# Head-wise attention backward on one core: ScalarE's order around the exponential, and the queue of the first weight loads

## The chip, the cores and the metric

One Trainium2 chip, one core of it. The metric is device microseconds of one execution, the median of several; lower is better. The kernel before took 420.46 us (three runs, 419.29 to 421.68).

## What is computed

One token passes a layer that mixes a cached attention block and a dense block with a gate, and the gradients of everything but `B_x` are returned with it. All tensors are bf16; `x` is 640 wide, there are 32 heads of 128, and each head's cache holds 4096 keys and 4096 values.

```python
def _A_ref(x, k_cache, v_cache, wq, wo):
    q = (x @ wq).reshape(B, Sq, H, Dh).transpose(0, 2, 1, 3)
    scores = einsum("bhqd,bhkd->bhqk", q, k_cache) * (Dh ** -0.5)
    p = softmax(scores)
    o = einsum("bhqk,bhkd->bhqd", p, v_cache)
    return o.transpose(0, 2, 1, 3).reshape(B, Sq, H * Dh) @ wo

g = sigmoid((x * gate_w).sum(-1))
out = g * _A_ref(...) + (1 - g) * _B_ref(...)      # _B_ref: w1, bias, Mish, w2
_out, _vjp = jax.vjp(_f, A_x, A_k_cache, A_v_cache, A_wq, A_wo, B_w1, B_b1, B_w2, gate_w)
return (_out, *_vjp(grad_out))
```

The large data are K and V in (32 MB each) and dK and dV out (32 MB each). For one head, dV is the outer product of the probabilities p with the gradient of the head's output, and dK that of ds = p * (dP - D) with the scaled query, where dP = V · dO.

## The kernel before

**Tiling.** A head's K (or V) is one SBUF tile of 128 partitions by 32 rows by 128 elements, 1 MB, loaded by one DMA on SP's queue. There are four buffers for K, three for V, and four for finished outputs `o_sb` (1 MB each). Four heads make a group; a group has a 640 KB slice of `wq` and one of `wo`.

**One head.** `tr_block` turns a quarter of K or V (8 of the 32 rows) with TensorE into one of two PSUM buffers `tr`, and ScalarE copies that to `KT` or `VT` (line 449). So V of a head is four blocks, `v_tr(h, 0)` to `v_tr(h, 3)`, and block 2 can only be transposed once block 0 is copied out. `scores` multiplies KT with the query; VectorE takes the row maximum `m` and ScalarE makes the diagonal `dgm` of it. `softmax` lets TensorE spread the maxima (`mx`, line 480), VectorE reduce them to `negM` (line 482), and ScalarE take the exponential `e_bf` (line 485), with a second short instruction that reads its row sum into `zd`. `dP` multiplies VT with dO on TensorE; VectorE's `pj` (line 492) multiplies dP with `e_bf`. `zd_mm` (line 496) sums over the partitions, `probs` (lines 500 to 506) makes p and ds, `dv_out` and `dk_out` make the outputs with two VectorE products each (line 511) and store each 1 MB with one DMA on SP's queue. `dq_o` (line 534) reads K and V once more on TensorE, and `dqo_red` (line 543) collects its result.

**The order around the change.** The order is written by hand: each engine runs its instructions in the order of the program's text. In the loop over the heads (from line 623) it is: V blocks 0 and 1, `softmax(h)` with the exponential, `dk_out(h - 1)`, for the first head of a group `g_dobc` (one TensorE product and one ScalarE copy to `do_row`), V blocks 2 and 3, `dP(h)`, K blocks 0 and 1 of the next head, `zd_mm`, `probs`, K blocks 2 and 3, `dv_out`, `scores(h + 1)`, `dq_o(h)`, then the loads of K four heads on and V three heads on, and then `dqo_red` and other work that fills in (weight gradients of the group before, the dense block). On ScalarE, the copies of V blocks 2 and 3 therefore stand behind the exponential, which waits for VectorE's `negM`. The last head stands by itself (from line 709) with the same order.

**Start.** SP issues the two halves of K of head 0 (line 130), then V of 0, K of 1, V of 1, K of 2, `wq` and `wo` of group 1, V of 2, K of 3, and the dense weights. POOL issues `wq` and `wo` of group 0 (lines 131 and 132), then a small bias load, and after these it makes the identity matrix (lines 153 and 154) and clears buffers. The first use of `wq` is `g_qcol(0)` (line 585), the query columns of group 0; nearly all that follows on TensorE and VectorE in the prologue stands behind it. The first use of `wo` is `g_do(0, hh)` (lines 614 and 615, instruction in line 219), four VectorE reductions, one per head, that give dO; the row maximum of head 0 stands behind them on VectorE.

Of the kernel before, what the change touches and what calls it, by code (L numbers as in the profile page):

```python
# [16 lines left out]
def kernel(  # L17
# [24 lines left out]
    nc = tc.nc  # L42
# [66 lines left out]
    def load_v(h):  # L109
        if h < H:  # L110
            vts[h] = kv_in.tile([P, J, Dh], BF16, name="Vn", tag="Vn", bufs=VBUFS)
            nc.sync.dma_start(vts[h][:], Vv[h])

    def load_wq(g, eng):
        wqs[g] = wts.tile([P, RC, GD], BF16, name="wq_g", tag="wq_g")
        eng.dma_start(wqs[g][:], wq_v[:, :, g * GD:(g + 1) * GD])

    def load_wo(g, eng):
        wos[g] = wts.tile([P, G, D], BF16, name="wo_g", tag="wo_g")
        eng.dma_start(wos[g][:], wo_v[:, g * G:(g + 1) * G, :])  # L120
# [7 lines left out]
    kts[0] = kv_in.tile([P, J, Dh], BF16, name="Kn", tag="Kn")  # L128
    for c in range(2):
        nc.sync.dma_start(kts[0][:, c * JH:(c + 1) * JH, :], Kv[0][:, c * JH:(c + 1) * JH, :])  # L130
    load_wq(0, nc.gpsimd)
    load_wo(0, nc.gpsimd)
    load_v(0)
    load_k(1)
    load_v(1)
# [80 lines left out]
    def g_do(g, hh):  # L216
        gp = groups[g]
        junk = small.tile([P, D], BF16, name="junk", tag="junk", bufs=2)
        nc.vector.scalar_tensor_tensor(junk[:], in0=wos[g][:, hh, :], scalar=1.0, in1=da_bc[:],  # L219
                                       op0=ALU.mult, op1=ALU.mult, accum_out=gp["do_col"][:, hh:hh + 1])  # L220
# [17 lines left out]
    def g_dobc(g):  # L238
        g_bcast(groups[g]["do_diag"], groups[g]["do_row"], 0, G)
# [11 lines left out]
    def f_bc(g, a=0, b=G):  # L251
        g_bcast(groups[g]["dq_diag"], groups[g]["dq_bc"], a, b)

    def f_aT_pe(g, a=0, b=G):
        gp = groups[g]
        gp["aT_ps"] = grp([P, RC], F32, "aT_ps")
        for c in range(RC):
            for hh in range(a, b):
                nc.tensor.matmul(gp["aT_ps"][:, c:c + 1], lhsT=wos[g][:, hh, c * P:(c + 1) * P],
                                 rhs=gp["o_bf"][:, hh:hh + 1], start=(hh == a), stop=(hh == b - 1))  # L260
# [4 lines left out]
    def f_dx(g, c, a=0, b=G, slot=None):  # L265
        gp = groups[g]
        cs = slice(a * Dh, b * Dh)
        slot = g if slot is None else slot
        junk = small.tile([P, D], BF16, name="junk", tag="junk", bufs=2)
        nc.vector.scalar_tensor_tensor(junk[:, cs], in0=wqs[g][:, c, cs], scalar=1.0, in1=gp["dq_bc"][:, cs],  # L270
                                       op0=ALU.mult, op1=ALU.mult, accum_out=dx_parts[:, c, slot:slot + 1])
# [172 lines left out]
    def tr_block(src, dst, c):  # L444
        sl = slice(c * TB, (c + 1) * TB)
        tp = tr_ps.tile([P, TB, P], BF16, name="tr", tag="tr")
        for t in range(TB):
            nc.tensor.transpose(tp[:, t, :], src[:, c * TB + t, :], ident_bf[:])  # L448
        nc.scalar.copy(dst[:, sl, :].rearrange("p a b -> p (a b)").bitcast(F32),  # L449
                       tp[:].rearrange("p a b -> p (a b)").bitcast(F32))  # L450

    def cols_mm(out, T, zrow):
        for j in range(J):
            nc.tensor.matmul(out, lhsT=T[:, j, :], rhs=zrow[:, J - 1 - j:2 * J - 1 - j],  # L454
                             start=(j == 0), stop=(j == J - 1))

    def k_tr(h, c):
        if h < H:
            if c == 0:
                KT[h] = kvT.tile([P, J, P], BF16, name="KT", tag="KT")  # L460
            tr_block(kts[h], KT[h], c)

    def v_tr(h, c):
        if c == 0:
            VT[h] = kvT.tile([P, J, P], BF16, name="VT", tag="VT")
        tr_block(vts[h], VT[h], c)
# [11 lines left out]
    def softmax(h):  # L478
        mx = s_ps.tile([P, P + 2], F32, name="mx", tag="mx")
        nc.tensor.matmul(mx[:, 0:P], lhsT=scale_f[:], rhs=dgms.pop(h)[:], start=True, stop=True)  # L480
        negM = small.tile([P, 1], F32, name="negM", tag="negM")
        nc.vector.tensor_reduce(negM[:], mx[:, 0:P], axis=AX.X, op=ALU.max, negate=True)  # L482
        es[h] = small.tile([P, J], BF16, name="e_bf", tag="e_bf")
        zds[h] = small.tile([P, 2], F32, name="zd", tag="zd")
        nc.scalar.activation(es[h][:], S_ps.pop(h)[:], ACT.Exp, bias=negM[:], scale=scale, accum_out=zds[h][:, 0:1])  # L485
        return mx

    def dP(h):
        DP_ps[h] = s_ps.tile([P, J], F32, name="DP", tag="DP")
        cols_mm(DP_ps[h][:], VT.pop(h), doz[h // G % 2][:, h % G, :])  # L490
        pj = small.tile([P, J], F32, name="pj", tag="pj")
        nc.vector.scalar_tensor_tensor(pj[:], in0=DP_ps[h][:], scalar=1.0, in1=es[h][:],
                                       op0=ALU.mult, op1=ALU.mult, accum_out=zds[h][:, 1:2])

    def zd_mm(h, mx):
        nc.tensor.matmul(mx[:, P:P + 2], lhsT=ones_f[:], rhs=zds[h][:], start=True, stop=True)
# [19 lines left out]
    def out_pair(h, dst, col4, row):  # L516
        hh = h % G
        t = outs.tile([P, J, Dh], BF16, name="o_sb", tag="o_sb")
        for a in (0, JH):
            outer(t, col4, row[:, hh * Dh:(hh + 1) * Dh], a, a + JH)  # L520
            if h == H - 1:
                nc.sync.dma_start(dst[h][:, a:a + JH, :], t[:, a:a + JH, :])
        if h < H - 1:
            nc.sync.dma_start(dst[h], t[:])
# [4 lines left out]
    def dk_out(h):  # L529
        out_pair(h, dKv, ds4s[h], groups[h // G]["qs_row"])  # L530
# [92 lines left out]
    for h in range(H - 1):  # L623
        g, hh = h // G, h % G
        nx, pv = g + 1 < NG, g > 0
        v_tr(h, 0)
        v_tr(h, 1)
        mx = softmax(h)
        if h > 0:
            dk_out(h - 1)  # L630
        if hh == 0 and pv:
            g_dobc(g)
        v_tr(h, 2)
        v_tr(h, 3)
        dP(h)
        if hh == 0 and pv:
            f_bc(g - 1)
            f_aT_pe(g - 1)
        k_tr(h + 1, 0)
        k_tr(h + 1, 1)  # L640
        zd_mm(h, mx)
        if hh == 0 and pv:
            f_dx(g - 1, 0)
        if hh == 1 and pv:
            f_dx(g - 1, 3)
        if hh == 2 and nx:
            g_do(g + 1, 0)
        if hh == 3 and nx:
            g_do(g + 1, 3)
        probs(h, mx)  # L650
        k_tr(h + 1, 2)
        k_tr(h + 1, 3)
        dv_out(h)
        scores(h + 1)
        od = dq_o(h)
        load_k(h + KBUFS)
        load_v(h + VBUFS)
        dqo_red(h, od)
        budget = 0.0
        if hh == 0:  # L660
            if nx:
                g_new(g + 1)
            if pv:
                f_aT_add(g - 1)
                f_dx(g - 1, 1)
                f_dx(g - 1, 2)
                f_dwo(g - 1, 0)
                f_dwo(g - 1, 1)
            budget = 2.7
        if hh == 1:  # L670
            if pv:
                f_dx(g - 1, 4)
                for c in range(RC):
                    f_dwq(g - 1, c)
                f_dwq_st(g - 1)
                f_dwo(g - 1, 2)
                f_dwo(g - 1, 3)
                f_dwo_st(g - 1)
            if g + 2 < NG:
                load_wq(g + 2, nc.gpsimd if pv else nc.sync)  # L680
                load_wo(g + 2, nc.gpsimd if pv else nc.sync)
            budget = 1.8
        if hh == 2:
            if nx:
                g_do(g + 1, 1)
                g_do(g + 1, 2)
                g_qcol(g + 1)
            budget = 2.7
        if hh == 3:
            if nx:  # L690
                g_docol(g + 1)
                g_dodiag(g + 1)
                g_q(g + 1)
                g_qs(g + 1)
                f_new(g)
                f_diag(g)
            budget = 1.8
        if h >= 2:
            mlp_some(budget)
            dw2_some(2)  # L700
        if h == H - 4:
            assert not mq and dw2_next[0] == FCN
            nc.gpsimd.dma_start(dw1_v, w1_sb[:])
            for a, b in W2P:
                nc.gpsimd.dma_start(dw2_v[:, a:b, :], w2_sb[:, a:b, :])
            nc.gpsimd.dma_start(out_8[FM:F, :], w2_sb[0:FT, FR, :])
            nc.sync.dma_start(db1_row, dh_bc[0:1, :])

    g, h = NG - 1, H - 1
# [3 lines left out]
    nc.vector.tensor_tensor(gg[:], g_all[:], omg_all[:], ALU.mult)  # L713
    v_tr(h, 0)
    v_tr(h, 1)
    mx = softmax(h)
    f_new(g)
    l_new()
    f_diag(g, 0, 3)
    l_dqbf(0, 3)  # L720
    v_tr(h, 2)
    v_tr(h, 3)
    dP(h)
    zd_mm(h, mx)
    f_bc(g, 0, 3)
# [81 lines left out]
```

## Time and profile before

| | |
|---|---|
| median of three runs | 420.46 us (419.29 to 421.68) |
| the profiled execution's own time | 420.13 us |
| its span, first to last instruction | 418.4 us |
| TensorE matmul busy | 320.5 us, 77% |
| VectorE busy | 303.1 us, 72% |
| ScalarE busy | 216.3 us, 52% |
| POOL busy | 38.1 us, 9% |
| moved by DMA | 165.05 MB, mean 395 GB/s |
| granted TensorE clock, mean | 0.893 |

Busy times are shares of the whole span; stages differ, so the views by window and the waits count for more than these sums. A row of the view of waits reads: engine, tile and line that waited, what released it, us in total, times, and (for the whole core) the longest. A row of the view of groups ends with the idle time just before its instructions and what ended it. In the timeline a row is start, duration, engine, line, operation, tiles and count; in brackets stands idle time before it. In the view of windows each row has, after the engines' busy times, the granted clock, the share of time in which the 16 DMA engines had a packet, and GB/s. That share can pass 1 where packets overlap.

### The profile page before, as it was taken

To read this page: it belongs to the slowest core of one execution; us is meant where nothing else is said; L and a number is where in the kernel's file an instruction comes from. 1 tells how busy PE (TensorE), PEld (TensorE's weight loads), DVE (VectorE), ACT (ScalarE), POOL (GpSimd) and SP (SyncE) were. 2 spreads that over 40 slices of the span, in tenths; PEclk is the share of its full clock that TensorE was granted. 3 is DMA by queue.
4 is the path that set the end of the run, shared out by engine and by line. 5 is a ranking of instruction groups with operands and counts; after the bars stand their busy time and mean duration, and the time that the engine had idled before them with its cause. 6 is when DMAs were issued, how large, how long until landed. Compare 5 with 4: busy or idle time off the path is not lost.

```text
span 418.4 us, 15402 instructions
## 1 busy us (share of the span) xinstructions
PE 320.5 (77%) x6797; PEld 291.5 (70%) x6797; DVE 303.1 (72%) x816; ACT 216.3 (52%) x447; POOL 38.1 (9%) x61
## 2 busy tenths in 40 slices
PE   1598959888699779777987889777897888847850
PEld 1487838777679778767877778666787787747740
DVE  0536645787868987798869796888887987718681
ACT  2255434674346635455666764665445644545560
POOL 5000010001100100001104100001000040000120
PEclk9999898999789998888998898878988989959985
DMA  8999999999999999999999999999999999999956
GB/s 292 394 408 422 420 397 418 417 378 412 404 406 356 387 417 405 414 411 404 410 389 420 424 418 408 421 415 352 407 385 423 383 418 420 416 421 415 401 228 244
DMA packets 28074, 165.05 MB, mean 395 GB/s; under 512 B 3093, under 2 KB 5462, under 8 KB 12007
## 3 DMA queue, kind: packets, MB, share of 16 engines
q1 hardware_dynamic: 22402, 141.28, 83.7%
q0 software_dynamic: 5552, 22.79, 13.8%
q8 instruction: 53, 0.87, 0.8%
q14 instruction: 15, 0.11, 0.1%
q10 hardware_dynamic: 52, 0.01, 0.0%
HBM read 82.03 MB, written 82.03 MB: 392 GB/s over the span
## 4 chain that ended last, share of the span: by engine, by line
PE 39%; ACT 22%; DVE 20%; DMA 11%; issue 5%; DVEq 0%; POOL 0%; ACTq 0%; POOLq 0%
PE tr L448 16%; PE od L534 11%; ACT VT L449 8%; ACT KT L449 7%; DMA out_dram<-o_sb 6%; DVE o_sb L511 4%; DMA wo_g<-in_A_wo_dram 3%; PE S L454 3%; PE DP L454 3%; DVE junk L408 2%; PE q_ps L197 2%; DVE junk L219 2%; DVE junk L270 2%; DVE mjunk L430 2%; ACT e_bf L485 2%
## 5 line engine op out<-in xcount | busy, mean ns | idle before, releaser
L448 PE MATMUL tr<-ident_bf,Vn 128*128 128x128 bf16 x1024 | 78.8, 236 | 24.7 <-ACT VT L449 15.5
L449 ACT COPY KT<-tr 128x512 f32<-128x512 f32 x128 | 70.5, 587 | 48.7 <-PE tr L448 48.6
L448 PEld LDWEIGHTS <-Vn 128*128 128x128 bf16 x1024 | 70.4, 107 | 35.4 <-issue 25.3
L448 PE MATMUL tr<-ident_bf,Kn 128*128 128x128 bf16 x1024 | 83.5, 245 | 6.9 <-DMA Kn<-in_A_k_cache_dram 5.0
L448 PEld LDWEIGHTS <-Kn 128*128 128x128 bf16 x1024 | 76.9, 114 | 8.8 <-DMA Kn<-in_A_k_cache_dram 4.9
L449 ACT COPY VT<-tr 128x512 f32<-128x512 f32 x128 | 69.4, 586 | 23.4 <-PE tr L448 22.8
L511 DVE TENSOR_TENSOR o_sb<-qs_row,ds 128x2048 bf16<-128x2048 bf16 x64 | 78.1, 1263 | 2.9 <-DMA out_dram<-o_sb 2.9
L511 DVE TENSOR_TENSOR o_sb<-do_row,p 128x2048 bf16<-128x2048 bf16 x64 | 75.2, 1217 | 1.1 <-DMA out_dram<-o_sb 1.1
L454 PE MATMUL DP<-doz,VT 128*128 128x32 bf16 x1024 | 39.6, 179 | 27.9 <-ACT VT L449 24.1
L454 PEld LDWEIGHTS <-VT 128*128 128x128 bf16 x1024 | 33.2, 98 | 32.9 <-ACT VT L449 31.8
L454 PE MATMUL S<-qz,KT 128*128 128x32 bf16 x1024 | 36.9, 180 | 3.1 <-ACT KT L449 0.4
L476 ACT ACTIVATE dgm<-ident_bf,m 128x128 f32<-128x128 bf16 x32 | 12.9, 402 | 50.3 <-DVE m L474 50.3
L454 PEld LDWEIGHTS <-KT 128*128 128x128 bf16 x1024 | 32.4, 98 | 6.4 <-ACT KT L449 5.8
L534 PE MATMUL od<-p,Vn 128*128 128x32 bf16 x1024 | 31.5, 177 | 3.9 <-issue 3.9
L534 PE MATMUL od<-ds,Kn 128*128 128x32 bf16 x1024 | 31.2, 177 | 2.3 <-issue 2.3
L534 PEld LDWEIGHTS <-Vn 128*128 128x128 bf16 x1024 | 28.4, 96 | 4.4 <-issue 4.4
L534 PEld LDWEIGHTS <-Kn 128*128 128x128 bf16 x1024 | 28.3, 96 | 2.6 <-issue 2.6
L270 DVE SCALAR_TENSOR_TENSOR junk<-wq_g,dq_bc 128x512 bf16<-128x512 bf16 x35 | 23.5, 687 | 4.0 <-ACT dq_bc L233 4.0
L320 POOL DMA_DIRECT2D out_dram<-wq_g x8 | 7.1, 886 | 206.6 <-DVE wq_g L317 108.0
L219 DVE SCALAR_TENSOR_TENSOR junk<-wo_g,da_bc 128x640 bf16<-128x640 bf16 x32 | 25.5, 820 | 0.4 <-DMA wo_g<-in_A_wo_dram 0.4
L482 DVE TENSOR_REDUCE negM<-mx 128x1 f32<-128x128 f32 x32 | 9.2, 288 | 22.8 <-PE mx L480 22.7
L323 ACT ACTIVATE wo_g<-da_bc,dqo 128x640 bf16<-128x640 bf16 x32 | 24.5, 813 | 0.0
(157 smaller groups left out, 326.8 us busy)
## 6 DMA issues: line engine op xcount, KB each, us to landing
out_dram<-o_sb SPq DMA_DIRECT2D x62, 1024.0 KB, 10.4
Vn<-in_A_v_cache_dram SPq DMA_DIRECT2D x32, 1024.0 KB, 14.8
Kn<-in_A_k_cache_dram SPq DMA_DIRECT2D x31, 1024.0 KB, 15.5
out_dram<-wq_g POOLq DMA_DIRECT2D x8, 640.0 KB, 10.5
out_dram<-wo_g POOLq DMA_DIRECT2D x7, 640.0 KB, 14.2
wq_g<-in_A_wq_dram POOLq DMA_DIRECT2D x6, 640.0 KB, 11.7
wo_g<-in_A_wo_dram POOLq DMA_DIRECT2D x6, 640.0 KB, 12.1
w_sb<-in_B_w_dram SPq DMA_DIRECT2D x1, 2160.0 KB
```

The lines of the kernel that those rows point to most:

```text
L197: nc.tensor.matmul(ps[:], lhsT=x_col_bf[:, rc:rc + 1].to_broadcast([P, P]), rhs=wqs[g][:, rc, :], start=(rc == 0), stop=(rc == RC - 1))
L219: nc.vector.scalar_tensor_tensor(junk[:], in0=wos[g][:, hh, :], scalar=1.0, in1=da_bc[:], op0=ALU.mult, op1=ALU.mult, accum_out=gp["do_col ...
L270: nc.vector.scalar_tensor_tensor(junk[:, cs], in0=wqs[g][:, c, cs], scalar=1.0, in1=gp["dq_bc"][:, cs], op0=ALU.mult, op1=ALU.mult, accum_ ...
L323: nc.scalar.activation(wos[g][:, hh, :], da_bc[:], ACT.Copy, scale=groups[g]["dqo"][:, 1, hh:hh + 1])
L408: nc.vector.scalar_tensor_tensor(junk[0:n, :], in0=w2_sb[0:n, fc, :], scalar=dm[0:n, fc:fc + 1], in1=db_bc[0:n, :], op0=ALU.mult, op1=ALU. ...
L448: nc.tensor.transpose(tp[:, t, :], src[:, c * TB + t, :], ident_bf[:])
L449: nc.scalar.copy(dst[:, sl, :].rearrange("p a b -> p (a b)").bitcast(F32), tp[:].rearrange("p a b -> p (a b)").bitcast(F32))
L454: nc.tensor.matmul(out, lhsT=T[:, j, :], rhs=zrow[:, J - 1 - j:2 * J - 1 - j], start=(j == 0), stop=(j == J - 1))
L476: nc.scalar.activation(dgms[h][:], ident_bf[:], ACT.Copy, scale=m32[:])
L482: nc.vector.tensor_reduce(negM[:], mx[:, 0:P], axis=AX.X, op=ALU.max, negate=True)
L511: nc.vector.tensor_tensor(dst[:, a:b, :].rearrange("p j (k t) -> p j k t", t=4), row.rearrange("p (k t) -> p k t", t=4).unsqueeze(1).to_br ...
L534: nc.tensor.matmul(out, lhsT=N[:, j, :], rhs=c4[:, 4 * j:4 * j + W], start=(j == 0), stop=(j == J - 1))
```

## The change

In the loop and in the last head, `softmax` ends with `negM`; the exponential and its tiles become a function `exps`, called after V blocks 2 and 3. In the loop the small `g_dobc` of a group's first head now comes after `exps` as well. At the start, `wq` and `wo` of group 0 are no longer issued by POOL but by SP: `wq` after the first half of K of head 0, `wo` after the second.

```diff
     for c in range(2):
         nc.sync.dma_start(kts[0][:, c * JH:(c + 1) * JH, :], Kv[0][:, c * JH:(c + 1) * JH, :])
-    load_wq(0, nc.gpsimd)
-    load_wo(0, nc.gpsimd)
+        (load_wo if c else load_wq)(0, nc.sync)
     load_v(0)
...
         nc.vector.tensor_reduce(negM[:], mx[:, 0:P], axis=AX.X, op=ALU.max, negate=True)
+        return mx, negM
+
+    def exps(h, negM):
         es[h] = small.tile([P, J], BF16, name="e_bf", tag="e_bf")
         zds[h] = small.tile([P, 2], F32, name="zd", tag="zd")
         nc.scalar.activation(es[h][:], S_ps.pop(h)[:], ACT.Exp, bias=negM[:], scale=scale, accum_out=zds[h][:, 0:1])
-        return mx
...
         v_tr(h, 0)
         v_tr(h, 1)
-        mx = softmax(h)
+        mx, negM = softmax(h)
         if h > 0:
             dk_out(h - 1)
+        v_tr(h, 2)
+        v_tr(h, 3)
+        exps(h, negM)
         if hh == 0 and pv:
             g_dobc(g)
-        v_tr(h, 2)
-        v_tr(h, 3)
         dP(h)
...
-    mx = softmax(h)
+    mx, negM = softmax(h)
     f_new(g)
     l_new()
     f_diag(g, 0, 3)
     l_dqbf(0, 3)
     v_tr(h, 2)
     v_tr(h, 3)
+    exps(h, negM)
     dP(h)
```

## The prediction

> **What bounds the kernel now.** I read the view of windows first, because DMA is busy in nearly every slice of the page while the engines are not.
>
> ```profile
> 19.00:23.00 4.00, 2.67 (x8) 0.99 (x8) 1.28 (x8) 0.99 (x2) 0.00 (x0) 1.00 1.08 365
> 24.00:55.00 31.00, 27.57 (x609) 25.26 (x607) 18.57 (x44) 15.57 (x34) 0.00 (x0) 0.94 1.02 419
> 84.00:92.00 8.00, 7.23 (x189) 6.95 (x189) 6.70 (x15) 5.21 (x12) 0.00 (x0) 1.00 0.99 366
> 114.00:116.00 2.00, 1.88 (x63) 1.78 (x61) 2.00 (x3) 1.07 (x2) 0.00 (x0) 1.00 0.99 292
> 130.00:142.00 12.00, 11.64 (x299) 10.95 (x295) 10.94 (x31) 8.05 (x16) 0.00 (x0) 1.00 0.94 335
> 282.00:294.00 12.00, 9.31 (x194) 8.82 (x193) 10.53 (x26) 6.02 (x13) 1.63 (x2) 0.78 0.93 356
> 326.00:334.00 8.00, 7.35 (x186) 6.83 (x184) 7.44 (x19) 5.06 (x11) 0.00 (x0) 1.00 1.01 377
> 338.00:384.00 46.00, 33.82 (x750) 31.20 (x749) 29.32 (x79) 21.09 (x44) 1.93 (x4) 0.85 1.01 418
> ```
>
> The last column is GB/s. With a deep queue (24 to 55, 338 to 384) the DMA engines move 418; in 84 to 92, 130 to 142, 282 to 294 and 326 to 334 they move 335 to 377. Adding the bytes that SP's issues announce and taking off those moved, I find 4 to 6 MB waiting in the good stretches and only 0.4 to 2.5 MB in these four: there the queue runs low because the compute has not yet produced a store or freed a buffer. So compute and DMA are almost level, compute sets the pace until about 334 us, and DMA sets it from there to 387 us. The chain of waits says the same.
>
> ```profile
> 2.31 13.88 DMA wo_g<-in_A_wo_dram
> 16.29 3.07 DVE junk L219 x8
> ...
> 359.79 27.16 DMA out_dram<-o_sb
> ```
>
> Between the first weight load and 359.79 us the only DMA of size in that chain is one small `h_sb` copy of 5.33 us; the rest is TensorE, ScalarE and VectorE. The 27.16 us are a dK store standing in a full queue. Then the waits.
>
> ```profile
> ACT e_bf L485 <- DVE negM L482: 26.7, 19, 4.6
> DVE dqo L543 <- PE od L534: 26.0, 31, 2.1
> PE DP L454 <- ACT VT L449: 24.1, 16, 3.4
> PE tr L448 <- ACT VT L449: 15.5, 14, 3.8
> DVE rz L500 <- PE mx L496: 11.2, 20, 1.2
> PE tr L448 <- DMA Vn<-in_A_v_cache_dram: 7.7, 2, 6.6
> PE qc_ps L209 <- DMA wq_g<-in_A_wq_dram: 5.0, 1, 5.0
> ```
>
> ScalarE stands 26.7 us at the exponential, TensorE 39.6 us for copies of VT, and VectorE 37.2 us for TensorE's results further on. TensorE waits for a V load only in two places, at 372 and 384 us; after the very first K block no head before that waits for its K or V.
>
> **Part one, the first weights.** Now `wq` starts on POOL at 1.28 us, shares the DMA engines with SP's K and V, and `g_qcol` starts at 11.95; `wo` allows the first reduction at 16.29. On SP the queue order is half K, `wq`, half K, `wo`. The packets of the first half of K go out by 4.05 us and it is usable at 4.95, so 0.9 us lies between the two. `wq` as SP moved it for group 1 took 1.9 us, `wo` 1.8, half a K 1.3: out at 5.95, 7.25 and 9.05, usable at about 6.9, 8.2 and 10.0. The first K blocks and the small transposes hold TensorE to 7.0 and VectorE to 7.35, so `g_qcol` moves from 11.95 to about 7.3. The steps from it to the second `da_bc` product end at 15.9 today and then at 11.3; the reduction, no longer waiting for `wo`, starts at 11.35 in place of 16.29. The first V block moves from 22.84 to 17.9: **4.9 us earlier**. V of head 0 lands at about 12.4 instead of 10, K of head 1 at 15, both before use (17.9 and 22.3). POOL loses two issues of 1.03 and 0.79 us; the identity is there earlier, but the first transpose waits for K at 4.95 anyway: nothing. SP gets two more issues of some 0.45 us before V of 0, hidden by queued data.
>
> The price is in the packets. The trace's packet records show POOL moving these slices in packets of 4096 and 5120 bytes (medians 159 and 196 ns), SP in 1024 and 1280 (46 and 58 ns): 640 x 46 + 512 x 58 over 16 engines is 3.70 us, 160 x 159 + 128 x 196 is 3.16, so +0.5 us. The windows bound it below: 19 to 23, where SP moves such a pair, loses 4 x (1 - 365/419) = 0.5 us, and 5 to 16 with POOL's pair (397 GB/s) 0.6, so about -0.1. I take +0.3.
>
> The Trainium skill (DMA: Bandwidth & Descriptors, "Why small descriptors are slow") speaks against this edit: each packet costs about three extra cycles and 32 bytes of descriptor traffic whatever its size. By it, 864 more packets on 1.31 MB would cost an estimated 0.25 us, and the sum would read 414.35 instead of 414.4.
>
> **Part two, the exponential.** It removes and adds no instruction: 32 exponentials (0.29 us, plus 0.19 for the row sum) go behind two copies of 0.59. What it frees is seen in head 13.
>
> ```profile
> 182.19 0.28 DVE L482 TENSOR_REDUCE negM<-mx 128x1 f32<-128x128 f32 x1
> 182.39 2.35 DVE L511 TENSOR_TENSOR o_sb<-qs_row,ds 128x2048 bf16<-128x2048 bf16 x2
> 182.50 0.29 ACT L485 ACTIVATE e_bf<-S,negM 128x32 bf16<-128x32 f32 x1 [2.12 <-DVE negM L482]
> 182.78 1.06 ACT L449 COPY VT<-tr 128x512 f32<-128x512 f32 x2
> 183.41 0.85 PE L454 MATMUL DP<-doz,VT 128*128 128x32 bf16 x16 [1.98 <-ACT VT L449]
> ```
>
> VectorE is late with `negM` (fill-in work), ScalarE sits 2.12 us, and TensorE 1.98. With the new order the two copies run at 180.5 to 181.7, dP and K blocks 0 and 1 of the next head follow, all before `negM`. That alone wins nothing: `pj` stands behind VectorE's 2.35 us dK product either way. Two things shorten VectorE's loop. First, `zd_mm` stands behind the K blocks on TensorE and comes up to 2.1 us after `pj` starts, where 0.36 is the least: over 0.36 it is 0.8, 1.0, 1.8, 1.0, 1.4, 0.8, 0.8 and 1.05 us in heads 7, 8, 12, 16, 20, 21, 22 and 24, mostly first heads of a group, sum 8.6. Second, from `zd_mm` to the end of `od` is 4.9 us in heads 10, 11, 13, 14, 20, 21, 23 and 24, against 4.20 where the K copies were already done (heads 9, 15, 25): 8 x 0.7 = 5.6, and VectorE waits at `dqo` for just this. Together 14.2 us at most, 0 at least; nearest to head 13's row is the second alone, so I take half, 7.
>
> What is queued behind the waiting exponential now: the KT copies of the next head (and `do_row` in a group's first head). The exponential ends 0.4 us after `negM`, two KT copies 1.1 later; `zd_mm` cannot come before `negM` + 2.9, so they are covered by the dK product. For early `negM` the exponential ends 0.51 us after VT's last copy, dP and `pj` with its read at 0.7: covered too, by 0.2; without that cover each head would pay up to 0.48.
>
> **Sum.** Compute would be 4.9 + 7 = 12 us ahead by 334 us. DMA cannot give all that: it gives back only what it lost in the four thin stretches, 8 x (1 - 366/418) + 12 x (1 - 335/418) + 12 x (1 - 356/418) + 8 x (1 - 377/418) = 1.0 + 2.4 + 1.8 + 0.8 = 6.0 us. The rest of the lead turns into longer waits for V29 and its neighbours (6.6 us now). After V30 has landed (384.3) nothing changes: two heads and the last stores, 34 us; in heads 30 and 31 `negM` is early and the exponential covered. So 420.13 - 6.0 + 0.3 = 414.4 for the profiled execution; it stood 0.33 below the median, so **414.8**. Its own bounds: the start alone gives 4.9 less 0.5; if the small dips (407 GB/s average from 200 to 300, three POOL dips like that at 114) also go, up to 9 less 0. That is 411 to 416.5.
>
> **Rivals.** *The start alone counts.* If the late `negM`, not VT, sets each head (VectorE is 10.94 of 12 us busy in 130 to 142), part two gives 0: 420.46 - 4.9 + 0.3 = 415.9, 415.5 to 418. For it: in early heads block 2's copy follows block 1's by 0.2 us, so the exponential hid there. Against: the 37 us of VectorE's waits.
> *DMA is the whole bound.* The share of DMA is 0.98 to 1.04 in nearly all slices; if the thin stretches are slow for another reason (share 0.99 at 366 GB/s speaks for it), both gains become waits for loads and 0.3 to 0.5 remain: 420.9, no change. Against it: no head waits for K or V before 372 us, and 130 to 142 has share 0.94.
> *The exponential becomes the late one (slower).* Place: `pj` and the KT copies behind it. Price: 0.48 us in each of 32 heads, 15.4 if nothing covers, less 4.6 net from the start: 431; at half, 423.6. It decides from 0.21 us a head on (6.7 us in all). For it: the cover is 0.2 us. Against: the dK product starts with `negM` and lasts 2.35.
>
> **How the numbers follow.** Forecast 0.45; start alone 0.22; DMA the bound 0.18; exponential late 0.10; something unseen 0.05, slower for the most part. About 0.5%, 2.1 us, is what a measurement of this kernel can tell from no change: faster is under 418.4, slower over 422.6. The first two are faster (0.67), the third the same, the rest slower. The range is 411.0 to 420.5: below lies 0.05, above it the slow cases and part of the third.
>
> **What would show it.** Right: `g_qcol` near 7.3 and the first V block near 18; the ScalarE wait at the exponential still there, but TensorE's waits for VT gone to a few us; `zd_mm` 0.36 us after `pj`; the four thin stretches near 410 GB/s; longer waits for V29. Wrong: `pj` waiting for `e_bf`; K or V waits from 100 us on with the thin stretches still thin; a first V block later than 20 us.

## The result, and the profile after

The changed kernel takes **417.65 us** (median of 20 runs, 416.26 to 418.82) against 419.09 us (20 runs, 417.08 to 422.33) for the kernel before on the same chip. The ratio on record is 0.9954, 95% interval 0.9937 to 0.9972; the two medians alone give 0.9966. By the ratio that is a gain of 0.46%, 1.9 us, where 5.7 us were forecast. It is clear of zero, but less than the 2.1 us that the prediction took for the least that can be told from no change. The profiled execution took 418.82 us with a span of 417.1 us; it was 420.13 and 418.4 before.

First the windows that were shown of before, now of the changed kernel (engines' busy times, granted clock, DMA share, GB/s), and two late ones.

```profile
84.00:92.00 8.00, 6.95 (x178) 6.51 (x175) 7.50 (x19) 5.48 (x12) 1.70 (x2) 1.00 1.01 419
130.00:142.00 12.00, 9.74 (x248) 8.88 (x246) 11.46 (x28) 7.54 (x15) 1.63 (x2) 1.00 1.01 421
282.00:294.00 12.00, 10.06 (x229) 9.50 (x227) 10.99 (x25) 5.42 (x13) 2.00 (x3) 0.86 1.00 390
326.00:334.00 8.00, 6.89 (x159) 6.34 (x155) 6.88 (x22) 5.85 (x13) 4.51 (x7) 1.00 1.01 405
338.00:384.00 46.00, 32.77 (x630) 30.25 (x631) 24.38 (x65) 19.05 (x39) 0.00 (x0) 0.78 0.96 393
380.00:390.00 10.00, 8.92 (x224) 8.47 (x222) 8.98 (x24) 7.01 (x16) 1.69 (x2) 1.00 0.76 297
390.00:400.00 10.00, 9.24 (x256) 8.57 (x253) 6.81 (x22) 6.51 (x15) 0.00 (x0) 1.00 0.70 276
```

The four thin stretches are filled, the third and fourth not quite: 419, 421, 390 and 405 GB/s in place of 366, 335, 356 and 377. What was won there is lost again at the end: 338 to 384 falls from 418 to 393, and from 380 to 400 a quarter of the DMA engines' time and more is empty (shares 0.76 and 0.70). Before, these two windows of 380 to 400 were fuller:

```profile
380.00:390.00 10.00, 7.95 (x196) 7.30 (x193) 8.00 (x20) 6.34 (x13) 1.70 (x2) 1.00 1.01 416
390.00:400.00 10.00, 8.83 (x217) 8.00 (x215) 6.52 (x23) 5.64 (x13) 0.00 (x0) 1.00 0.81 327
```

Adding up the packets, the changed kernel has moved 2.2 MB more than the one before at 340 us, and the same at 400.

The waits of the changed kernel (engine, line, releaser: us, times, longest):

```profile
PE tr L447 <- DMA Vn<-in_A_v_cache_dram: 22.4, 11, 6.2
DVE dqo L544 <- PE od L535: 16.5, 28, 1.4
PE tr L447 <- ACT VT L448: 16.2, 12, 5.6
DVE pj L493 <- PE DP L453: 10.8, 6, 5.9
ACT e_bf L487 <- DVE negM L481: 7.4, 6, 3.5
DVE rz L501 <- PE mx L497: 6.6, 12, 1.0
```

dP no longer appears as waiting for VT (24.1 us before), and ScalarE waits 7.4 us at the exponential in place of 26.7. TensorE's wait for VT at `tr` stays (16.2 us, 15.5 before). In place of the waits that are gone TensorE waits 22.4 us for V loads, in 11 places, against 7.7 in two. The first of the 11 is at 144.2 us (V11), and 10.2 of the 22.4 us lie before 334. The chain of waits (start, duration, what) says the same:

```profile
317.10 22.62 DMA Vn<-in_A_v_cache_dram
339.79 32.98 DMA Vn<-in_A_v_cache_dram
372.81 1.89 PE tr L447 x16
```

The 32.98 us are V29. It is used at 372.81, although issued 3.1 us earlier than in the kernel before (339.79 against 342.93), where it was used at 372.06. Why it did not land earlier is in the semaphore events: every such load raises its semaphore sixteen times. These are the sixteen times for V29, in us, read from the trace's semaphore events:

```
before  361.5 362.2 362.4 362.6 362.8 362.8 363.0 363.4 363.4 363.9 364.1 364.5 364.9 365.0 365.9 372.0
after   355.1 355.3 355.3 355.3 355.6 356.2 356.4 356.5 357.9 357.9 358.9 359.4 360.9 364.9 365.7 372.8
```

The middle of the sixteen (their median) comes 6.2 us earlier (363.4 to 357.2), about the 6.0 us of the prediction. The last comes 0.8 us later, and TensorE waits for the last. It is not V29 alone: from V10 to V29 the middle comes 1.2 to 6.4 us earlier in the changed kernel and the last 0.7 to 6.9 us later. How far the last increment is behind the middle one is called the lag from here on. The Trainium skill (DMA: Bandwidth & Descriptors, "Why a DMA increments its semaphore by 16 and not by 1") says that each increment is one DMA engine reporting its own share, and that only the full count means that all has landed. By this reading one engine is late, and the change did not make it faster. The experiments test this reading against its rivals.

### The profile page after: what moved, and what is told of

Same layout as the page of the kernel before. It is cut to its first block, busy times and chain, and to the rows that moved or that the text cites. A ratio compares the mean times of both kernels' runs of the same rounds, so it can differ in the third digit from the quotient of the medians.

```text
span 417.1 us, 15399 instructions
## 1 busy us (share of the span) xinstructions
PE 318.8 (76%) x6797; PEld 286.6 (69%) x6797; DVE 301.2 (72%) x816; ACT 216.1 (52%) x447; POOL 36.4 (9%) x59
## 4 chain that ended last, share of the span: by engine, by line
DMA 39%; PE 29%; DVE 14%; ACT 11%; issue 3%; POOL 1%; DVEq 0%; SPq 0%; ACTq 0%; POOLq 0%
DMA Vn<-in_A_v_cache_dram 32%; PE tr L447 13%; PE od L535 7%; DVE o_sb L512 5%; DMA out_dram<-o_sb 5%; ACT KT L448 5%; ACT VT L448 4%; PE S L453 2%; DMA h_sb<-dh_bc 2%; PE DP L453 2%; DVE junk L218 1%; PE mx L479 1%; PE q_ps L196 1%; ACT wo_g L322 1%; PE mx L497 1%
## 5 line engine op out<-in xcount | busy, mean ns | idle before, releaser
L447 PE MATMUL tr<-ident_bf,Vn 128*128 128x128 bf16 x1024 | 82.5, 243 | 40.0 <-DMA Vn<-in_A_v_cache_dram 22.4
L447 PEld LDWEIGHTS <-Vn 128*128 128x128 bf16 x1024 | 73.8, 111 | 51.5 <-DMA Vn<-in_A_v_cache_dram 25.6
L448 ACT COPY KT<-tr 128x512 f32<-128x512 f32 x128 | 69.3, 587 | 49.0 <-PE tr L447 48.9
L512 DVE TENSOR_TENSOR o_sb<-qs_row,ds 128x2048 bf16<-128x2048 bf16 x64 | 76.2, 1232 | 9.9 <-DMA out_dram<-o_sb 9.8
L447 PE MATMUL tr<-ident_bf,Kn 128*128 128x128 bf16 x1024 | 76.0, 232 | 8.9 <-POOL h_sb L337 5.3
L447 PEld LDWEIGHTS <-Kn 128*128 128x128 bf16 x1024 | 69.5, 107 | 11.0 <-issue 5.4
L475 ACT ACTIVATE dgm<-ident_bf,m 128x128 f32<-128x128 bf16 x32 | 12.9, 402 | 57.3 <-DVE m L473 57.3
L453 PE MATMUL DP<-doz,VT 128*128 128x32 bf16 x1024 | 35.7, 179 | 2.2
L453 PEld LDWEIGHTS <-VT 128*128 128x128 bf16 x1024 | 31.9, 97 | 5.8 <-ACT VT L448 4.1
L535 PEld LDWEIGHTS <-Vn 128*128 128x128 bf16 x1024 | 28.6, 97 | 2.4 <-issue 2.4
L535 PEld LDWEIGHTS <-Kn 128*128 128x128 bf16 x1024 | 28.4, 97 | 0.7 <-issue 0.6
L497 PE MATMUL mx<-zd,ones_f 128*128 128x2 f32 x64 | 12.6, 266 | 18.1 <-DVE pj L493 18.1
```

What stands on the lines that cost most here:

```text
L475: nc.scalar.activation(dgms[h][:], ident_bf[:], ACT.Copy, scale=m32[:])
L512: nc.vector.tensor_tensor(dst[:, a:b, :].rearrange("p j (k t) -> p j k t", t=4), row.rearrange("p (k t) -> p k t", t=4).unsqueeze(1).to_br ...
L535: nc.tensor.matmul(out, lhsT=N[:, j, :], rhs=c4[:, 4 * j:4 * j + W], start=(j == 0), stop=(j == J - 1))
```

## The experiments

They ran on four chips, each with runs of the kernel before beside them; the ratios are to those. Times inside a kernel come from one trace of it.

**The two parts alone.** The start alone: the exponential stays where it was, and only this is changed of the kernel before.

```diff
     for c in range(2):
         nc.sync.dma_start(kts[0][:, c * JH:(c + 1) * JH, :], Kv[0][:, c * JH:(c + 1) * JH, :])
-    load_wq(0, nc.gpsimd)
-    load_wo(0, nc.gpsimd)
+        (load_wo if c else load_wq)(0, nc.sync)
```

> Start alone: wq and wo of group 0 on SP, the exponential where it was. My theory now (one of the 16 DMA engines is behind the others from about 80 us on and sets the end; the compute's lead feeds only the other fifteen): 0.3 to 1.5 us faster than before, ratio 0.996 to 0.999, first V block at about 18 us, and the last of the 16 increments of late V loads 7 us or more after the fifteenth. The prediction's theory (the start's 4.9 us reach the end, since DMA had lost 6 us in thin stretches): 4 to 5 us faster, ratio 0.988 to 0.990.

Measured: 418.84 us, ratio to before 1.0001 (0.9975 to 1.0027). The first V block starts at 18.23 us, 4.6 us earlier, and the first two thin stretches are filled (420 and 420 GB/s; the other two have 373 and 383); nothing of it that can be measured reaches the end. V29's middle increment comes at 360.0, 3.4 us earlier than before, but V29 is used at 373.85, 13.8 us behind that middle.

The exponential alone, the start as before (the rest of the edit stands under The change):

```diff
     v_tr(h, 2)
     v_tr(h, 3)
+    exps(h, negM)
```

> Exponential behind the V copies alone, wq and wo of group 0 on POOL as before. Slowest-engine theory: 0.3 to 1.5 us faster than before, ratio 0.996 to 0.999, so the two parts do not add up. The prediction's theory: 3 to 6 us faster (0.986 to 0.993), a lead of about 7 us by 334 us. If the exponential itself were worth nothing: ratio 1.000 and TensorE's waits for VT unchanged.

Measured: 416.86 us, ratio 0.9968 (0.9947 to 0.9990). First V block at 23.07, the four thin stretches at 400, 399, 420 and 417 GB/s, V29 at 371.33. What gain there is comes from this part, and the start adds nothing that can be measured.

**Which engine is late.** Small loads of k rows behind the big ones show it. In the trace a load of k rows leaves one increment at its issue and then k later ones. The first of two kernels has them at heads 14, 22 and 26, with 12, 8 and 4 rows:

```diff
+        if h in (14, 22, 26):
+            for k in (12, 8, 4):
+                nc.sync.dma_start(probe[(h, k)][:], Kv[0][0:k, 0, 0:64])
```

> The changed kernel with nine tiny extra loads on SP's queue (12, 8 and 4 partitions of 128 bytes, after the V loads of heads 14, 22 and 26; their data are not used). If one fixed DMA engine is behind, the probes that run on it land with the straggler and those that do not land 5 us or more earlier at head 26, so that the probes tell apart which quarter of the engines it is in (or that it is in none of the first twelve). If the whole queue is late, all three land within 2 us of the last increment of the V load ahead of them. Time within 1 us of the changed kernel.

The second has 7, 6 and 5 rows, at heads 18 and 26.

> The changed kernel with six tiny extra loads on SP's queue (7, 6 and 5 partitions of 128 bytes, after the V loads of heads 18 and 26; their data are not used). The first probes put the two latest engines behind the probe of 8 partitions and not behind that of 4. Each of the three should now land either with the latest (within 0.5 us of the V load's last increment) or 1 us or more earlier; from the smallest that still lands with it follows which of the four it is. Time within 1 us of the changed kernel.

They took 419.15 and 420.04 us, one run each, which is 1.5 and 2.4 us over the changed kernel where under 1 was expected. Last two increments in us, behind the V load of the same head (k = 12, 8, 4 in the first kernel; 7, 6, 5 in the second):

```
head 26  V29  370.31 371.84   k=12 370.51 372.04   k=8 370.73 372.24   k=4 359.84 365.72
head 26  V29  368.91 373.00   k=7  369.33 373.21   k=6 359.11 373.41   k=5 359.50 373.60
head 18  V21  264.31 267.73   k=7  264.51 267.93   k=6 260.38 268.13   k=5 258.28 268.33
```

The latest increment is there with five rows and gone with four; the second latest is there with seven and gone with six. It is the same at heads 18 and 26, and at heads 14 and 22 the latest is gone with four rows too. The page and section named above say that a load of k rows issued by SP runs on the k lowest-numbered engines. By it the late engine is always the fifth, and the next the seventh. Neither the trace nor these runs name an engine.

**Does the late engine set the time?** The changed kernel with one extra load in each of 24 heads, read by nobody: four rows of it in one kernel, five in the other.

```diff
         load_v(h + VBUFS)
+        if 4 <= h < 28:
+            nc.sync.dma_start(extra[5 * (h - 4):5 * (h - 4) + 4, :], Kv[h][0:4, 0:24].rearrange("p j d -> p (j d)"))
```

> The changed kernel with one extra load each at heads 4 to 27, behind the V load: 4 rows of K of 6 KB each, into a tile nobody reads. Four rows go to the first four of the sixteen DMA engines, and not to the fifth, the late one: 24 times 6 KB at the 26 GB/s an engine makes in the profiled stretches of 420 GB/s is 5.6 us more for each of these four, and nothing for the late one. If the late engine sets the landing of the V blocks and the end: 417.0 to 419.0 us (417.65 for the changed kernel), the last increment of V29 not over 1 us later. Rival, the sum of all bytes sets the end: 0.59 MB at 420 GB/s, 1.4 us more, 419.0. Rival, any four engines made later set the end: up to 5.6 us more.

> The same with 5 rows in place of 4, so that the fifth engine, the late one, gets 24 times 6 KB too. If the late engine sets the end: 5.6 us more for it, 421.5 to 424.0 us, the last increment of V29 4 to 6 us later than with four rows. Rival, the sum of bytes: 0.74 MB, 1.8 us more than the changed kernel, 419.4, and only 0.4 us more than with four rows.

Measured on one chip: with four rows 417.62 us, ratio 0.9942 (0.9921 to 0.9964); with five 423.89, ratio 1.0098 (1.0070 to 1.0126). **0.59 MB that pass the late engine by cost nothing that can be measured, and 0.15 MB more, on the late one, cost 6.3 us.** The last increments of V29:

```
4 rows  ... 359.4 359.4 360.1 360.2 365.8 370.5
5 rows  ... 362.5 362.5 363.0 363.0 364.5 376.9
```

Only the last one moves far, by 6.4 us; the middle one goes from 359.3 to 361.9. The chain of waits of the kernel with five rows goes through two V loads, V28 and V30:

```profile
333.51 29.82 DMA Vn<-in_A_v_cache_dram
...
368.58 18.97 DMA Vn<-in_A_v_cache_dram
```

The sum of the bytes as the bound gave 419.0 and 419.4 us; the measured pair differs by 6.3, so that theory falls.

**Bytes taken from in front of V29.** The stores of the MLP's weight gradients (4.4 MB) go on SP's queue behind the last V load, in place of POOL's.

```diff
-            nc.gpsimd.dma_start(dw1_v, w1_sb[:])
+            nc.sync.dma_start(dw1_v, w1_sb[:])
...
-                nc.gpsimd.dma_start(dw2_v[:, a:b, :], w2_sb[:, a:b, :])
-            nc.gpsimd.dma_start(out_8[FM:F, :], w2_sb[0:FT, FR, :])
+                nc.sync.dma_start(dw2_v[:, a:b, :], w2_sb[:, a:b, :])
+            nc.sync.dma_start(out_8[FM:F, :], w2_sb[0:FT, FR, :])
```

> The changed kernel with the stores of the dense weight gradients (4.4 MB) on SP's queue behind the last V load in place of POOL's queue. Slowest-engine theory: V of head 29 lands 6 to 10 us earlier (its share of the engines is not halved any more), but the end stays within 2 us of the changed kernel, since the late engine has the same bytes to move. Rival (the dense stores in the way of V28 to V30 took back the lead): the end 4 to 8 us earlier, 410 to 413 us.

Measured: 418.04 us, ratio 0.9985 (0.9962 to 1.0009). V29 is used at 359.90, 12.9 us earlier than in the changed kernel, and the end stays. The chain of this kernel now ends in a store:

```profile
377.56 19.94 DMA out_dram<-o_sb
397.50 0.02 issue
397.53 2.36 DVE o_sb L512 x2
```

VectorE stands until 397.50 for a buffer whose store has its middle increment at 385.2 and its fifteenth at 388.8: the last engine is 8.7 us behind the fifteenth. In its windows (columns as above) the compute engines stand still from 390 to 397.5:

```profile
380.00:390.00 10.00, 7.99 (x194) 7.08 (x191) 2.47 (x16) 6.90 (x14) 0.72 (x1) 0.99 0.76 308
390.00:400.00 10.00, 0.00 (x0) 0.00 (x0) 2.47 (x5) 0.00 (x0) 0.05 (x1) 0.50 0.62 250
```

The edit changes the order of the transfers, not their bytes. The wait moved from a load to a store.

**What makes it late: the group transfers of POOL?** The group loads and stores of the weights go from POOL to SP.

```diff
-        nc.gpsimd.dma_start(dwq_v[:, :, g * GD:(g + 1) * GD], wqs.pop(g)[:])
+        nc.sync.dma_start(dwq_v[:, :, g * GD:(g + 1) * GD], wqs.pop(g)[:])
...
-        nc.gpsimd.dma_start(dwo_v[:, g * G + a:g * G + b, :], wos[g][:, a:b, :])
+        nc.sync.dma_start(dwo_v[:, g * G + a:g * G + b, :], wos[g][:, a:b, :])
...
+            if g + 2 < NG and pv:
+                load_wq(g + 2, nc.sync)
+                load_wo(g + 2, nc.sync)
```

> The changed kernel with the weight-gradient stores and all weight loads of the groups on SP's queue (loads of later groups two heads later than now), so that up to the dense stores at about 334 us POOL issues no large DMA. If POOL's transfers (their descriptors, or their own ring) make one engine late: the last of the 16 increments of V loads between 200 and 330 us comes within 2 us of the fifteenth and within 4 us of the median. If the instruction fetches do (53 of 16 KB, about 1.0 us each on one engine): as now, the last 8 to 14 us behind the median. Time within 2 us of the changed kernel either way, since SP's queue gets more to wait for.

Measured: one run, 418.62 us, against 419.34 for the kernel before. The lag of V29 falls to 4.2 us, but its last increment is still at 371.2, because the middle comes later too: V29 is issued only at 356.8 us (339.8 in the changed kernel). So moving these transfers doesn't help the end. On the way they do count. From V17 to V25 the lag is 3.9 to 4.6 us, where it is 7.2 to 14.1 in the changed kernel. At V20 and V21 the middle comes at nearly the same time in both (245.2 and 245.5, 259.0 twice), and the last comes 7.8 and 4.1 us earlier, with all 53 instruction fetches in place. That is near what was expected if POOL's transfers make the engine late. It is one trace, with some loads moved by two heads, so a part of POOL in the lag is likely and its size not shown.

**Or the instruction fetches?** The profile lists them as a queue of their own (`q8 instruction`). With 2 of the 32 matmuls in each chain there are fewer instructions to fetch; the other 30 are left out, so these kernels compute only a part of the sums.

```diff
-        for j in range(J):
-            nc.tensor.matmul(out, lhsT=T[:, j, :], rhs=zrow[:, J - 1 - j:2 * J - 1 - j],
-                             start=(j == 0), stop=(j == J - 1))
+        for j in range(2):
+            nc.tensor.matmul(out, lhsT=T[:, j * (J - 1), :], rhs=zrow[:, J - 1 - j * (J - 1):2 * J - 1 - j * (J - 1)],
+                             start=(j == 0), stop=(j == 1))
```

> The changed kernel with 2 of 32 matmuls in each of the four chains scores, dP, dq and o of every head (the other 30 are left out, so these sums are wrong), which leaves about half of the instructions and the same 165 MB of DMA. If the instruction fetches make the late engine late: about 24 to 28 fetches in place of 53, the last increment of late V loads 4 to 8 us behind the median in place of 12 to 16, and the end 6 to 12 us earlier than the changed kernel (405 to 411 us). If the engine is late for another reason: the same lag of 12 us or more, and the end within 4 us of the changed kernel, since its bytes are the same.

Measured: one run, 408.28 us; 23 fetches for 53; V29 landed at 363.3, its lag 6.6 us. But TensorE had less to do as well. So the same with two wide matmuls put ahead of each chain:

```diff
+    def filler(big, T):
+        for _ in range(2):
+            nc.tensor.matmul(big[:, 2 * W:512], lhsT=T[:, 0, :],
+                             rhs=T[:, 0:4, :].rearrange("p a b -> p (a b)")[:, 0:512 - 2 * W], start=True, stop=True)
```

> The kernel with 2 of the 32 matmuls of each chain (scores, dP, dq, o; the other 30 are left out), but with two matmuls of 448 columns ahead of each chain, written where nobody reads, so that TensorE's time per chain stays near the 0.78 us of the full one: the instructions are few, the compute as slow as in the changed kernel. If the instruction fetches (53 in the changed kernel, 23 with the short chains) make the late engine late: some 25 fetches, the last increment of V29 at 362 to 366 us (372.8 in the changed kernel, 363.4 with the short chains), lag of it behind the median 5 to 9 us, time 408 to 412. Rival, the gain with the short chains came from faster compute: the last increment of V29 at 370 to 373, lag 13 to 16 us, 416 to 418.

Measured: 410.27 us, ratio 0.9798 (0.9761 to 0.9836). The row of the fetch queue (packets, MB, share of 16 engines), in the changed kernel:

```profile
q8 instruction: 53, 0.87, 0.8%
```

and in the kernel with the stand-ins:

```profile
q8 instruction: 25, 0.41, 0.4%
```

V29's increments in the latter are these:

```
348.7 348.8 350.2 350.5 350.8 353.5 354.9 355.9 357.4 357.6 359.4 359.5 359.6 361.6 362.3 364.1
```

The middle stays (356.6, against 357.2 in the changed kernel); the last one comes **8.7 us earlier**, 1.8 us behind the fifteenth in place of 7.0. From V29 to the end it is 43.2 us, against 44.3, so most of the gain is that of the late engine. The stand-ins give back only part of the compute (TensorE busy 275.5 us, 255.7 without them, 318.8 in the changed kernel). Two things speak against faster compute as the cause. The two short kernels differ by 19.8 us of TensorE's busy time, and V29's last increment by only 0.8 (363.3 and 364.1). And the start alone, which brought the compute 4.6 us forward, brought V29's last increment no earlier (373.8, 372.0 before). So the fetches are the likelier cause, but no run changed them alone. They took 53.7 us in all and then 25.8: 28 us fewer bring 8.7, so they are not simply added to the one engine. How they are spread over the engines the trace doesn't show.

**Relief for the late engine.** If four-row loads pass it by, part of each second V block can go that way: 112 rows in one DMA, 16 in four.

```diff
-            nc.sync.dma_start(vts[h][:], Vv[h])
+            if h >= 12 and h % 2 == 0:
+                nc.sync.dma_start(vts[h][0:112], Vv[h][0:112])
+                for p in range(112, P, 4):
+                    nc.sync.dma_start(vts[h][p:p + 4], Vv[h][p:p + 4])
+            else:
+                nc.sync.dma_start(vts[h][:], Vv[h])
```

> The changed kernel with ten V loads (every second head from 12 to 30) cut: 112 rows in one DMA and the last 16 rows in four DMAs of 4 rows, which go to the first four engines. The late engine moves 8 KB less of each of the ten loads (7 rows for 8): 10 times 0.31 us, 3.1 us; the first four move 9.4 us more. If the late engine sets the end and the first four stay ahead of it: 414.5 to 416.5 us, last increment of V29 2 to 3 us earlier. Rival, the sum of bytes (it is the same) or the work on one engine that is not the late one sets the end: 417.65 or more, with 40 more DMAs to issue on SP 418 to 419.

Measured: 433.53 us, ratio 1.0336 (1.0297 to 1.0374). SP's own waits in this kernel:

```profile
SPq L115 <- DMA Vn<-in_A_v_cache_dram: 30.1, 10, 3.7
SPq L115 <- DMA out_dram<-o_sb: 27.1, 17, 2.3
SPq L115 <- DMA Kn<-in_A_k_cache_dram: 25.2, 10, 3.6
```

Line 115 is the small load. It waits 82 us for transfers that it doesn't depend on by its data. In this program the DMA instructions of SP and ScalarE take eight semaphores in turn, each waits until the DMA that had its semaphore before has landed, and the trace never has more than eight of them in flight. Forty small DMAs each hold one of the eight places that a 1 MB transfer had; the rate falls to 366 GB/s from 260 to 310 us, against 398. A second try, with the small DMAs on ScalarE:

```diff
+        if 10 <= h + 2 < H and h % 2 == 0:
+            for p in range(112, P, 4):
+                nc.scalar.dma_start(vts[h + 2][p:p + 4], Vv[h + 2][p:p + 4])
```

> The cut V loads again (16 rows of every second V block from head 10 on in four DMAs of 4 rows, on the first four engines; 11 blocks), with the small DMAs issued by ScalarE behind the exponential two heads ahead of their use, so that SP issues no more than in the changed kernel. The late engine moves 7 rows of these blocks for 8: 11 times 0.31 us, 3.4 us less. If the late engine sets the end: 414.5 to 416.5 us, last increment of V29 2 to 3.5 us earlier. Rival, the bytes as a whole set it: 417.65; rival, ScalarE's 44 issues (0.3 us each, 1.2 us in every second head) land on the path: 418 to 420.

Measured: 441.63 us, ratio 1.0535 (1.0501 to 1.0570). The same eight semaphores serve both queues, and now ScalarE stands too: 36.1 us at `do_row` for a dV or dK store, once 14.9 us. My expectation missed this limit both times. No version here that computes the whole result beats the changed kernel beyond the intervals.

## Why the prediction was wrong

**Part one, the first weights: right in mechanism and size, no weight in the sum.** `g_qcol` starts at 7.5 us (7.3 said), the first V block at 18.06 (17.9 said). The price in packets is there as 863 more packets, too small to be seen in the time. The 4.8 us won there were worth nothing by the end that can be measured.

**Part two, the exponential: mechanism right, the term undersized.** I took 7 us out of 0 to 14.2. Over the 0.36 us that the prediction took as the least, `zd_mm` came 15.1 us behind the start of `pj` before and comes 8.0 now, summed over all heads: 7.1 less. From `zd_mm` to the end of `od` it is 7.7 us less: 14.8 together, a little over the upper bound. VectorE's wait at `dqo` fell from 26.0 to 16.5 us. Of the sign "TensorE's waits for VT gone to a few us" only half came: gone at dP, 16.2 us left at `tr`.

**The step that failed** is the middle of the sum: "DMA cannot give all that: it gives back only what it lost in the four thin stretches", 6.0 us. The stretches were filled, or nearly, and V29's middle increment came 6.2 us earlier, as worked out. The step took sixteen engines for one resource with one rate. A load lands with its slowest engine, and that one ran at its own pace: V29's last increment is at 372.0 before, 372.8 after, 373.8 with the start alone, 371.3 with the exponential alone. The 6.2 us went to engines that then stood empty (shares 0.76 and 0.70). What is left of it is at V30, whose last increment moved from 384.3 to 382.9 us, and the span is 1.3 shorter. The premise of the step, that compute sets the pace until 334 us and gets 12 us ahead by then, did not come either: in the changed kernel TensorE waits for V loads from 144 us on.

The trace of before already had it, though less: 372.0 against 365.9 for the fifteenth. I saw that V29 waited, and took the queue as a whole for the cause. "After V30 has landed (384.3) nothing changes" was right: from V30's use to the end of the span it was 34.0 us before and 33.9 after.

**The rivals.** "The start alone counts" (415.9) is the nearest to the time and the furthest from the truth, since the start alone gives 1.0001. "DMA is the whole bound" (420.9) had the right ending, both gains becoming waits for loads, on a wrong condition: it asked for thin stretches that stay thin, and they filled. "The exponential becomes the late one" did not come: `pj` still waits for dP (10.8 us), and not for `e_bf`.

**What stays open:** why it is these engines that are late, and how much of the lag comes from the fetches, from POOL's transfers or from something else.

## What to carry to other kernels

Before counting on DMA time, look at the last increment of the late loads beside the middle one: where they lie apart, the bound is the slowest engine, and GB/s and the share of DMA, being means over sixteen, hide it. Filling a thin stretch gains little if the transfer that is waited for is held by an engine that the filling brings no further. And before cutting a transfer into small ones, count how many may be in flight: each takes a place from a large one.

## What the runs showed of the hardware

- The sixteen DMA engines drift apart over this kernel: the last increment of V20 came 11.3 us behind the middle one in the changed kernel, and that of V28 19.5 us, where that of V2 came 1.6. In the kernel before it was 2.9 and 6.2 us.
- Load on the late engine is paid in full: 24 times 6 KB on it cost 6.3 us (5.6 expected), and as much on each of four others cost nothing that can be measured.
- With 25 instruction fetches of 16 KB in place of 53, V29 landed 8.7 us earlier. TensorE also had 43 us less to do in that kernel, so the fetches are the likelier cause, not the only one possible.
- With the group transfers on SP in place of POOL, the lag from V17 to V25 was 3.9 to 4.6 us, against 7.2 to 14.1 (one trace).
- Eight DMAs at a time, over the queues of SP and ScalarE together, is all that this program has in flight; forty more small ones made the kernel some 16 us slower (433.53 against 417.65).
